# Attention and a feed-forward layer in one kernel: another order of seven products at the hand-over, and operands of the second token pair made earlier

## The chip, the cores and the metric

One core of one Trainium2 chip. The metric is the device time of one execution in microseconds: 650.89 us, the median of three runs of the kernel before (649.39, 650.89 and 652.63).

## The reference

```python
# attention, B=4 H=8 S=576 D=64
scores = q @ k.T / sqrt(D) + bias(h, i, j)     # bias: a small MLP of log1p|i-j| / log1p(max(i,1))
attn = softmax(scores); x = attn @ v           # regrouped to x[2304 tokens, 512]
# feed-forward, d_ff = 2048
h = x @ w_in                                   # 512 -> 2048
g = s * relu(h)**2 + b
out = g @ w_out                                # 2048 -> 512
```

All in float32; the weights come as 64-bit floats and are decoded on the chip.

## The kernel before

**Attention.** 16 pairs (a head and two batches) go through the chip in `step(n)`, five steps a pair. The program is written out by hand: each engine gets its instructions in the order in which the Python code issues them, and works them off in that order. Pair 15 is the last; its results reach x as `rb` tiles (L443, L444), which are stored and read back as the last input block.

**Feed-forward.** x stands transposed, features by tokens, in three token pairs p of 768 tokens (two chunks of 384). The hidden width is cut into four groups g. An item is (g, p); the order of items is (0,0), (0,1), (0,2), (1,2) and so on, 12 in all. For one item the 2x2 block product (features halved, tokens halved) is made with seven products in place of eight, on sums of blocks: `W_OPS` and `X_OPS` name the operands, S1 to S4 sums of weights, T1 to T4 sums of x. Every float32 operand is split into a high and a low part, so that a product is six matmuls of 128x384 (`product`, L625 to L637: three combinations, two feature blocks). An item has two halves s, each with the seven products on other weight columns. So an item is 14 slots: slot T does product `ORDER[i]` of half s with n, r = divmod(T, 14) and s, i = divmod(r, 7); from the second item on, slots with i = 1, 4 and 6 also do 12 matmuls each of the output projection of the half before (L741). The first item has no projections beside it. A product is added on one of four PSUM banks (`BANK`, L457): 1 and then 2 on "a", 5 and then 3 on "b", 6 on "c", 7 and then 4 on "d".

**The posts of a half** (`quad_posts`, L640) take the banks apart. In the names used below: *keep* (ACT, L657) copies bank a after product 1 and before product 2 is added to it; *u2* (DVE, L661) adds that copy to bank c; *v* (DVE, L666) adds u2 to bank b after product 5 and before product 3 is added to it; *c22* (DVE, L669) adds bank d after product 7 and before product 4 is added to it; *relu11* (ACT, L680) reads bank a after product 2. Relu, square, affine, high and low (L684 to L716) turn the four results into the high and low part of g.

**Making an operand of x** is a cast of two blocks to the high part on ACT (*x_hi*, L594, two instructions) and two subtractions for the low part on DVE (*x_lo*, L598); T sums are two more DVE instructions each (L585). `prep` does this for the seven operands of pair 0 while the last two steps of attention run; `fresh_x` (L1025) posts it for pair 1 into slots 6 to 14 and for pair 2 into slots 20 to 28. GpSimd makes pair 0's T sums.

**Order of work.** `at(slot, fn, prio)` collects the posts of a slot, and `fire(slot)` issues them after the slot's products, by priority: posts that free banks have 0, the other posts 1, making operands 2. A product, and a post, waits by semaphore for what it reads or overwrites. The first four products stand by hand between the last steps of attention (L990 to L998); the loop at L1104 goes on with slot 4. The SP queue issues the DMAs in program order, stores of made operands (L603) among them.

Space: `xp` holds seven operand buffers, an eighth (`x7`) is made once the attention's buffers are closed (L1000).

Of the kernel before, what the change touches and what calls it, by code (L numbers as in the profile page):

```python
# [26 lines left out]
def attention_moe(ctx, tc, q, k, v, w_in, w_out, dist, par, out):  # L27
# [310 lines left out]
    def probs_t(n):  # L338
        p, t = divmod(n, 5)
        if p not in pts:  # L340
            pts[p] = (ptp.tile([128, 4, 2, S], F32, tag="pt", name="pt"),
                      ptp.tile([128, S], F32, tag="ptr", name="ptr"))
# [113 lines left out]
    ORDER = (1, 6, 5, 7, 2, 3, 4)  # L456
# [98 lines left out]
    xo, free_x, x_free = {}, [], [[], None]  # L555
# [37 lines left out]
    def x_hi(p, m, e):  # L593
        nc.scalar.activation(xo[p, m][:, 0, e], x_view(p, X_OPS[m], e), AF.Copy)  # L594

    def x_lo(p, m, e, free):
        t = xo[p, m]
        nc.vector.tensor_tensor(t[:, 1, e], x_view(p, X_OPS[m], e), t[:, 0, e].bitcast(F32), op=ALU.subtract)  # L598
        if isinstance(X_OPS[m], str):
            used((p, X_OPS[m], e), free)  # L600
# [24 lines left out]
    def product(n, s, m, last):  # L625
        g, p = items[n]
        b = BANK[m]
        if m in (1, 5, 6, 7):
            banks[n, s, b] = ps_h.tile([128, 512], F32, tag="h", name="hps")
        ps = banks[n, s, b][:, 0:CH]  # L630
        first = m in (1, 5, 6, 7)
        for i in range(6):
            k, e = divmod(i, 3)
            w, x = ((0, 0), (0, 1), (1, 0))[e]
            nc.tensor.matmul(ps, w_ops[m][:, w, k, s], xo[p, m][:, x, k], start=(first and i == 0),  # L635
                             stop=(i == 5), skip_group_check=not first)
        if last:  # L637
            free_x.append(xo.pop((p, m)))

    def quad_posts(n, s):  # L640
# [69 lines left out]
        def low(fo, j):  # L710
# [35 lines left out]
    def acc_of(p, i):  # L746
        if p != 1:
            return mix["acc" if p == 0 else "acc2"][i][:, 0:DM]
        f = big.bitcast(F32)
        return f[:, i, 0:512] if i < 4 else f[:, 2 * i - 8:2 * i - 6, 512:768]  # L750
# [173 lines left out]
    pctx = ExitStack()  # L924
    ptp = pctx.enter_context(tc.tile_pool(name="ptp", bufs=2, side="right", reuse_waits="tile"))
    scratch = [ptp.tile([128, 512], F32, tag="ws", name=f"ws{i}", bufs=4) for i in range(4)]
# [40 lines left out]
    def prep(m):  # L967
        x_new(0, m)
        for e in range(2):
            x_hi(0, m, e)  # L970
        for e in range(2):
            x_lo(0, m, e, x_free[e])

    next(att)
    for a in range(KB):
        load_x(1, a, 0, 2 * CH if a < KB - 1 else CH)
    next(att)
    for i in range(3):
# [39 lines left out]
    x_free[:] = [[t[:, 0:CH] for t in mix[e]] for e in ("acc", "acc2")]  # L1018
# [6 lines left out]
    def fresh_x(n, q, free):  # L1025
        base = 14 * n
        for a in range(KB) if q > 1 else ():
            at(base + 2, lambda a=a: load_x(q, a))
        for o, name in ((6, "T1"), (7, "T2"), (9, "T3"), (12, "T4")):
            for e in range(2):  # L1030
                at(base + o, lambda name=name, e=e: x_sum(q, name, e, nc.vector, free))
        for i, m in enumerate(ORDER):
            o = base + (7 + i if i > 0 else 6)
            at(o, lambda m=m: x_new(q, m))
            for e in range(2):
                at(o, lambda m=m, e=e: x_hi(q, m, e))
            for e in range(2):
                at(o + 1, lambda m=m, e=e: x_lo(q, m, e, free))
            if isinstance(X_OPS[m], str):
                at(o + 2, lambda m=m: store_x(q, m))  # L1040

    def fresh_w(g):
# [36 lines left out]
        for name, o in (("S1", 35), ("S2", 35), ("S3", 38), ("S4", 40)):  # L1079
# [8 lines left out]
    fresh_x(0, 1, x_free[0])  # L1088
    fresh_x(1, 2, x_free[1])
# [87 lines left out]
```

## Time and profile before

| | us |
|---|---|
| median of three runs | 650.89 |
| the profiled execution | 650.64 |
| its span on the core | 648.9 |
| PE busy | 631.1 (97%) |
| DVE, ACT, POOL busy | 511.4, 450.9, 165.6 |

The page gives one execution. The busy shares are means over the attention (the first 262 us) and the feed-forward layer (the rest). PE is busy nearly all the time, so its idle stretches and the stretches at the lower TensorE clock are what is left to read; the 40 slices of the page show one place with both in mid-span, at the change from attention to feed-forward.

### The profile page before, as it was taken

Reading aid. Unit: us, or ns where it says so; the run is one execution under the profiler, and the core shown is the slowest. Engines: PE = TensorE matmul, PEld = TensorE weight load, DVE = VectorE, ACT = ScalarE, POOL = GpSimd, SP = SyncE. Lnnn points to the kernel's source line nnn. Section 1 sums busy time; section 2 is a strip of 40 time slices with the busy share of each in tenths; the row PEclk is TensorE's granted clock in tenths of the full one; section 3 lists DMA queues with packets and bytes.
Section 4 is the critical chain, followed back from the end, with each engine's and each line's share of the span. In section 5 each row is a group of like instructions: output and inputs, shape, how many; then the busy total and the mean of one; then the engine's idle time right before and its main releaser. Section 6 shows DMA issues by size and latency. Waiting matters only on the chain.

```text
span 648.9 us, 14523 instructions
## 1 busy us (share of the span) xinstructions
PE 631.1 (97%) x5418; PEld 511.6 (79%) x5418; DVE 511.4 (79%) x1093; ACT 450.9 (69%) x945; POOL 165.6 (26%) x196
## 2 busy tenths in 40 slices
PE   8999999999999999979999999999999999999997
PEld 5667666666666666879898899999888999998886
DVE  7988889999999988897887566698686698575542
ACT  7988787888888788687676685576574665655540
POOL 7991423345697524010010100010100100000000
PEclk9999999999999999979999999999999999999999
DMA  6988777775776565693522445421627210718112
GB/s 187 327 249 248 260 245 236 246 235 183 255 245 220 170 205 159 219 368 110 223 92 89 168 164 177 164 88 34 239 95 251 90 58 1 268 48 280 62 48 98
DMA packets 51058, 115.27 MB, mean 178 GB/s; under 512 B 10156, under 2 KB 18860, under 8 KB 50988
## 3 DMA queue, kind: packets, MB, share of 16 engines
q1 hardware_dynamic: 50652, 114.08, 52.6%
q8 instruction: 43, 0.70, 0.4%
q10 hardware_dynamic: 208, 0.26, 0.1%
q14 instruction: 27, 0.22, 0.1%
q0 software_dynamic: 128, 0.00, 0.0%
HBM read 83.59 MB, written 30.14 MB: 175 GB/s over the span
## 4 chain that ended last, share of the span: by engine, by line
PE 75%; DMA 7%; POOL 5%; ACT 5%; DVE 4%; issue 3%; SPq 1%; DVEq 0%; ACTq 0%; POOLq 0%
PE o L741 31%; PE hps L635 27%; PE bps L168 5%; PE xps L437 5%; PE sps L275 4%; PE tps L348 3%; ACT pr L308 3%; DMA qt<-in_q_dram 2%; DMA kt<-in_k_dram 2%; DVE tt L297 1%; DMA rs<-rt 1%; POOL kr L248 1%; DMA big<-in_moe_w_in_dram 1%; DVE pt L378 1%; ACT pt L376 1%
## 5 line engine op out<-in xcount | busy, mean ns | idle before, releaser
L741 PE MATMUL o<-wo,gt 128*128 128x512 f32 x864 | 209.2, 392 | 0.0
L635 PE MATMUL hps<-x,wi 128*128 128x384 f32 x1008 | 190.7, 340 | 3.3 <-DVE h L666 3.3
L635 PEld LDWEIGHTS hps<-x,wi 128*128 128x128 f32 x1008 | 180.8, 190 | 10.0 <-DVE h L666 3.6
L741 PEld LDWEIGHTS o<-wo,gt 128*128 128x128 f32 x864 | 161.2, 188 | 31.3
L308 ACT ACTIVATE pr<-tt,mn 128x576 f32<-128x576 f32 x144 | 110.7, 770 | 35.4 <-DVE mn L297 35.2
L297 DVE CUSTOM_DVE_ANT_0 tt<-sps,bt 128x576 f32<-128x576 f32 x128 | 91.4, 751 | 8.4 <-PE sps L275 6.7
L348 PEld LDWEIGHTS tps<-ident,pr 64*128 64x128 f32 x1216 | 44.8, 137 | 44.2 <-issue 18.7
L437 PE MATMUL xps<-pt,vt 128*64 128x256 f32 (+1 forms) x512 | 76.0, 418 | 1.0 <-PE xps L437 1.0
L275 PE MATMUL sps<-kr,qr 64*128 64x288 f32 x768 | 73.2, 307 | 1.0 <-POOL kr L248 0.8
L348 PE MATMUL tps<-ident,pr 64*128 64x64 f32 x1216 | 56.7, 229 | 5.2 <-ACT pt L376 2.8
L275 PEld LDWEIGHTS sps<-kr,qr 64*128 64x128 f32 x768 | 58.8, 186 | 2.4 <-POOL kr L248 1.0
L699 ACT ACTIVATE h<-h,sb 128x384 f32<-128x384 f32 x72 | 50.8, 706 | 12.0 <-DVE h L695 10.8
L493 POOL TENSOR_SCALAR wf<-wf 128x512 f32<-128x512 f32 x16 | 13.0, 813 | 160.8 <-ACT wf L491 160.6
L378 DVE COPY pt<-tps 128x512 f32<-128x512 f32 x64 | 43.9, 685 | 9.1 <-PE tps L348 8.8
L680 ACT ACTIVATE h<-hps 128x384 f32<-128x384 f32 x24 | 11.7, 487 | 54.5 <-PE hps L635 54.5
L437 PEld LDWEIGHTS xps<-pt,vt 128*64 128x64 f32 x512 | 31.3, 136 | 21.3 <-issue 9.4
L716 DVE TENSOR_TENSOR gt<-h,gt 128x384 fp32r<-128x384 f32 x72 | 40.0, 557 | 6.1 <-ACT gt L707 6.0
L168 PE MATMUL bps<-f,pt__125 128*32 128x79 f32 (+44 forms) x640 | 39.7, 390 | 2.0 <-POOL f L137 1.2
L707 ACT ACTIVATE gt<-h 128x384 fp32r<-128x384 f32 x72 | 37.9, 526 | 2.3
L135 DVE TENSOR_SCALAR f<-lg,thr 128x432 f32<-128x432 f32 (+9 forms) x68 | 39.3, 659 | 0.0
L168 PEld LDWEIGHTS bps<-f,pt__125 128*32 128x32 f32 x640 | 24.1, 109 | 17.7 <-issue 6.4
L376 ACT ACTIVATE pt<-tps 128x512 f32<-128x512 f32 x64 | 36.8, 575 | 0.0
(145 smaller groups left out, 823.6 us busy)
## 6 DMA issues: line engine op xcount, KB each, us to landing
x<-xs SPq DMA_DIRECT2D x24, 768.0 KB
bias<-stg SPq DMA_DIRECT2D x36, 295.5 KB
xs<-x SPq DMA_DIRECT2D x12, 768.0 KB
bt<-bias SPq DMA_DIRECT2D x7, 1152.0 KB
kt<-in_k_dram SPq DMA_DIRECT2D x16, 464.0 KB
wd<-in_moe_w_out_dram SPq DMA_DIRECT2D x12, 512.0 KB
x<-xt SPq DMA_DIRECT2D x28, 192.0 KB
qt<-in_q_dram SPq DMA_DIRECT2D x16, 320.0 KB
```

Source lines behind the costliest of these rows:

```text
L168: nc.tensor.matmul(pb[32 * c:32 * c + 32, base + a:base + b], w2bd, mov, start=True, stop=True)
L275: nc.tensor.matmul(o, a, b, start=(i == 0), stop=(i == 2))
L297: nc.vector.tensor_tensor_reduce(tt.rearrange("p (a b) -> p a b", a=2), ps[x][:, :, 0:HALF], bias.rearrange("p (a b) -> p a b", a=2), -1.0 ...
L308: nc.scalar.activation(pr[:, x], tts.pop((n, x)), AF.Exp, bias=mn[:, x:x + 1], scale=-1.0, accum_out=sums[p][:, col // 3, col % 3:col % 3 ...
L348: nc.tensor.matmul(outs[r], src[d], ident[d, d], is_transpose=True, start=start, stop=True, skip_group_check=not start)
L376: nc.scalar.activation(o, i, AF.Copy)
L378: nc.vector.tensor_copy(o, i)
L437: nc.tensor.matmul(o, vt[:, 4 * x + kb, :], pt[:, kb, x, c], start=(i == 0), stop=(i == 4))
L635: nc.tensor.matmul(ps, w_ops[m][:, w, k, s], xo[p, m][:, x, k], start=(first and i == 0), stop=(i == 5), skip_group_check=not first)
L699: return lambda: nc.scalar.activation(tmp[fo, j], tmp[fo, j], AF.Identity, bias=b_, scale=s_)
L716: nc.vector.tensor_tensor(lo, tmp[fo, j], hi, op=ALU.subtract)
L741: nc.tensor.matmul(os_t[t], gt[:, a, tok], w[:, b], start=(fo == 0 and i == 0), stop=(fo == 3 and i == 2))
```

## The change

The order of the seven products becomes 1, 6, 2, 5, 7, 3, 4, and the posts of a half move to new slots with it: keep stays in slot 1 of the half and u2 in 2, relu11 goes from 5 to 3, v from 3 to 4, c22 from 4 to 5. The operand of product 1 of pair 0 is made on GpSimd ahead of the last steps of attention. Two operand buffers ("guests") and x7 are made as soon as the buffer of attention pair 14 is free, for which the pool of these buffers is split in two. In them the operands 1, 5 and 2 of pair 1, and the sum T1, are made by hand between the first four products. What is left of pair 1 is posted into slots 4 to 11, each operand's casts and subtractions in one slot (`x_make`); pair 2 goes to slots 18 to 27, its loads from slot 16 to 14. When the guests are done their room takes accumulators of pair 2.

```diff
-    ORDER = (1, 6, 5, 7, 2, 3, 4)
+    ORDER = (1, 6, 2, 5, 7, 3, 4)
...
         return (
-            (1, 0, keep), (2, 0, u2), (3, 0, v), (4, 0, c22),
-            (5, 1, relu11), (5, 1, square11), (5, 1, relu(f1, 1)), (5, 1, square(f1, 1)),
-            (6, 0, c12), (6, 1, square_v(f0, 1)), (6, 1, affine(f1, 1)), (6, 1, high(f1, 1)), (6, 1, high(f0, 0)),
-            (7, 0, c21), (7, 1, low(f1, 1)), (7, 1, low(f0, 0)), (7, 1, affine(f0, 1)), (7, 1, high(f0, 1)),
-            (7, 1, relu(f1, 0)),
+            (1, 0, keep), (2, 0, u2), (3, 0, relu11), (4, 0, v), (5, 0, c22), (6, 0, c12), (7, 0, c21),
+            (3, 1, square11), (4, 1, high(f0, 0)),
+            (5, 1, low(f0, 0)), (5, 1, relu(f1, 1)), (5, 1, square(f1, 1)),
+            (6, 1, square_v(f0, 1)), (6, 1, affine(f1, 1)), (6, 1, high(f1, 1)),
+            (7, 1, low(f1, 1)), (7, 1, affine(f0, 1)), (7, 1, high(f0, 1)), (7, 1, relu(f1, 0)),
...
+    def x_make(q, m, free):
+        x_new(q, m)
+        for e in range(2):
+            x_hi(q, m, e)
+        for e in range(2):
+            x_lo(q, m, e, free)
+
+    prep(1, nc.gpsimd, nc.gpsimd)
     next(att)
...
-    for m in ORDER:
+    for m in ORDER[1:]:
         prep(m)
...
+    x_sum(1, "T1", 0, nc.vector, sums1)
+    x_sum(1, "T1", 1, nc.vector, sums1)
+    x_make(1, 1, sums1)
     next(att)
     store_xt(NP - 1)
     copy_x()
     fire(1)
-    product(0, 0, 5, False)
+    product(0, 0, ORDER[2], False)
     fire(2)
-    product(0, 0, 7, False)
+    x_make(1, 5, sums1)
+    product(0, 0, ORDER[3], False)
     fire(3)
-    pctx.close()
+    x_make(1, 2, sums1)
...
-    fresh_x(0, 1, x_free[0])
-    fresh_x(1, 2, x_free[1])
+    at(4, lambda: store_x(1, 5))
+    fresh_x(1, sums1, ((4, "T2"), (6, "T3"), (7, 6), (8, 7), (9, "T4"), (10, 3), (11, 4)))
+    for a in range(KB):
+        at(14, lambda a=a: load_x(2, a))
+    fresh_x(2, [t[:, 0:CH] for t in fulls + new_f],
+            ((18, "T1"), (18, 1), (19, "T2"), (20, 6), (21, 2), (22, 5), (23, "T3"), (24, 7), (25, "T4"), (26, 3), (27, 4)))
```

How the queues stand, at the three places that matter. In these rows `x_...` is an operand buffer, `acc_...` a T sum of pair 1, `wd` the input of pair 1, `hps` a bank.

DVE in the first half of the first item, before: the last subtractions of pair 0, the last eviction of attention (L443, L444), then u2 (L661), v (L666), c22 (L669).

```order
L598 TENSOR_TENSOR x_5186<-ws_1026,x_5186 128x384
L598 TENSOR_TENSOR x_5186<-h_5262,x_5186 128x384
L443 TENSOR_TENSOR rb<-xps,rb 128x256
L444 TENSOR_TENSOR rb<-xps,rb 128x320
L661 TENSOR_TENSOR h_5262<-hps,h_5262 128x384
L666 TENSOR_TENSOR h_5263<-hps,h_5262 128x384
L669 TENSOR_TENSOR h_5263<-hps,h_5263 128x384
L684 SCALAR_TENSOR_TENSOR h_5263<-h_5263,sb 128x384
```

The same place now (the lines are three further on: u2 is L664, v L669, c22 L672, the square L687).

```order
L586 TENSOR_TENSOR acc_5329<-wd 128x384
L586 TENSOR_TENSOR acc_5330<-wd 128x384
L599 TENSOR_TENSOR x_5272<-wd,x_5272 128x384 x2
L444 TENSOR_TENSOR rb<-xps,rb 128x256
L445 TENSOR_TENSOR rb<-xps,rb 128x320
L664 TENSOR_TENSOR h_5276<-hps,h_5276 128x384
L599 TENSOR_TENSOR x_5273<-acc_5329,x_5273 128x384
L599 TENSOR_TENSOR x_5273<-acc_5330,x_5273 128x384
L687 SCALAR_TENSOR_TENSOR h_5277<-h_5277,sb 128x384
L599 TENSOR_TENSOR x_5274<-wd,x_5274 128x384 x2
L669 TENSOR_TENSOR h_5277<-hps,h_5276 128x384
```

Four instructions came in ahead of the eviction, and four subtractions and the square between u2 and v; the two T2 sums and c22 follow v.

ACT from the relu after c22 of the first half (L687) to keep of the second half (L657), before.

```order
L687 ACTIVATE h_5263<-h_5263 128x384
L690 ACTIVATE h_5263<-h_5263 128x384
L699 ACTIVATE h_5263<-h_5263,sb 128x384
L707 ACTIVATE gt_5376<-h_5263 128x384
L705 ACTIVATE gt_5377<-h_5263,sb 128x384
L594 ACTIVATE x_5385<-wd 128x384 x2
L699 ACTIVATE h_5263<-h_5263,sb 128x384
L707 ACTIVATE gt_5378<-h_5263 128x384
L687 ACTIVATE h_5262<-h_5262 128x384
L657 ACTIVATE h_5261<-hps 128x384
```

The same place now (relu L690, keep L660).

```order
L690 ACTIVATE h_5277<-h_5277 128x384
L693 ACTIVATE h_5277<-h_5277 128x384
L702 ACTIVATE h_5277<-h_5277,sb 128x384
L710 ACTIVATE gt_5396<-h_5277 128x384
L702 ACTIVATE h_5277<-h_5277,sb 128x384
L710 ACTIVATE gt_5397<-h_5277 128x384
L690 ACTIVATE h_5276<-h_5276 128x384
L511 ACTIVATE x_5183<-acc_5331 128x384
L511 ACTIVATE x_5183<-acc_5332 128x384
L660 ACTIVATE h_5275<-hps 128x384
```

One high (L705) went out of the row; two casts stand in it as before, now of operand 6.

DVE in the second half of the first item from u2 (L661) to v (L666), before.

```order
L661 TENSOR_TENSOR h_5261<-hps,h_5261 128x384
L716 TENSOR_TENSOR gt_5379<-h_5262,gt_5379 128x384
L585 TENSOR_TENSOR acc_5391<-wd 128x384
L585 TENSOR_TENSOR acc_5392<-wd 128x384
L598 TENSOR_TENSOR x_5180<-acc_5389,x_5180 128x384
L598 TENSOR_TENSOR x_5180<-acc_5390,x_5180 128x384
L666 TENSOR_TENSOR h_5261<-hps,h_5261 128x384
```

The same place now, from the two subtractions ahead of u2 (L664) to v (L669).

```order
L599 TENSOR_TENSOR x_5184<-acc_5333,x_5184 128x384
L599 TENSOR_TENSOR x_5184<-acc_5388,x_5184 128x384
L664 TENSOR_TENSOR h_5275<-hps,h_5275 128x384
L719 TENSOR_TENSOR gt_5398<-h_5276,gt_5398 128x384
L586 TENSOR_TENSOR acc_5329<-wd,acc_5331 128x384
L586 TENSOR_TENSOR acc_5330<-wd,acc_5332 128x384
L687 SCALAR_TENSOR_TENSOR h_5275<-h_5275,sb 128x384
L599 TENSOR_TENSOR x_5185<-wd,x_5185 128x384 x2
L669 TENSOR_TENSOR h_5276<-hps,h_5275 128x384
```

Between u2 and v stood five instructions and now stand six; the two subtractions of operand 7 are ahead of u2, whose casts on ACT stand behind keep.

## Rows read from the trace of the kernel before

**Rows 1.** The page: busy time of PE, and the granted clock in 40 slices.

```profile
PE 631.1 (97%) x5418; PEld 511.6 (79%) x5418; DVE 511.4 (79%) x1093; ACT 450.9 (69%) x945; POOL 165.6 (26%) x196
...
PEclk9999999999999999979999999999999999999999
```

**Rows 2.** Waits of PE: line, who is waited for, total us, times, longest.

```profile
PE hps L635 <- DVE h L666: 3.3, 1, 3.3
```

**Rows 3.** Windows: length, busy PE, PEld, DVE, ACT, POOL; clock; DMA share, GB/s.

```profile
278.60:279.20 0.60, 0.00 (x0) 0.00 (x0) 0.60 (x2) 0.60 (x2) 0.00 (x0) 0.56 0.97 321
280.00:285.00 5.00, 5.00 (x17) 5.00 (x16) 4.97 (x11) 4.25 (x10) 0.00 (x0) 0.50 0.95 367
285.50:286.00 0.50, 0.50 (x5) 0.50 (x4) 0.50 (x2) 0.50 (x2) 0.12 (x1) 1.00 1.03 430
290.00:340.00 50.00, 50.00 (x253) 45.27 (x251) 40.78 (x80) 35.53 (x72) 5.17 (x6) 1.00 0.41 152
```

**Rows 4.** Timeline of PE: start, length, instruction, count, [idle before <- releaser].

```profile
265.20 0.96 PE L635 MATMUL hps<-x,wi 128*128 128x384 f32 x4
265.83 10.28 PE L635 MATMUL hps<-x,wi 128*128 128x384 f32 x57
274.79 1.00 PEld L635 LDWEIGHTS hps<-x,wi 128*128 128x128 f32 x6 [0.28 <-ACT h L657]
279.44 6.85 PE L635 MATMUL hps<-x,wi 128*128 128x384 f32 x22 [3.33 <-DVE h L666]
289.23 3.31 PE L635 MATMUL hps<-x,wi 128*128 128x384 f32 x18
```

**Rows 5.** Timeline of DVE at the hand-over.

```profile
257.68 1.02 DVE L598 TENSOR_TENSOR x<-big,x 128x384 fp32r<-128x384 f32 x2
...
265.32 0.42 DVE L443 TENSOR_TENSOR rb<-xps,rb 128x256 f32<-128x256 f32 x1 [1.00 <-PE xps L437]
...
266.06 0.55 DVE L661 TENSOR_TENSOR h<-hps,h 128x384 f32<-128x384 f32 x1
266.71 0.56 DVE L666 TENSOR_TENSOR h<-hps,h 128x384 f32<-128x384 f32 x1
...
269.22 0.62 DVE L684 SCALAR_TENSOR_TENSOR h<-h,sb 128x384 f32<-128x384 f32 x1 [1.07 <-ACT h L680]
...
278.83 0.55 DVE L666 TENSOR_TENSOR h<-hps,h 128x384 f32<-128x384 f32 x1
```

**Rows 6.** Timeline of ACT at the hand-over.

```profile
268.69 0.49 ACT L680 ACTIVATE h<-hps 128x384 f32<-128x384 f32 x1 [4.99 <-PE hps L635]
269.08 0.52 ACT L687 ACTIVATE h<-h 128x384 f32<-128x384 f32 x1
...
270.93 0.53 ACT L707 ACTIVATE gt<-h 128x384 fp32r<-128x384 f32 x1
271.36 0.60 ACT L705 ACTIVATE gt<-h,sb 128x384 fp32r<-128x384 f32 x1
271.87 0.92 ACT L594 ACTIVATE x<-wd 128x384 fp32r<-128x384 f32 x2
274.27 0.47 ACT L657 ACTIVATE h<-hps 128x384 f32<-128x384 f32 x1
```

**Rows 7.** Timeline of POOL before the hand-over, and of POOL and DVE in the second item.

```profile
252.02 0.72 PE L282 MATMUL sps<-kt,qt 64*64 64x288 f32 x8
252.24 1.00 POOL L585 TENSOR_TENSOR h<-big 128x384 f32<-128x384 f32 x1 [3.44 <-ACT pr L308]
255.84 1.00 POOL L585 TENSOR_TENSOR h<-big,h 128x384 f32<-128x384 f32 x1 [0.55 <-PE tps L348]
...
317.46 0.96 POOL L493 TENSOR_SCALAR wf<-wf 128x512 f32<-128x512 f32 x1 [2.44 <-ACT wf L491]
317.86 1.43 DVE L598 TENSOR_TENSOR x<-acd,x 128x384 fp32r<-128x384 f32 x2
```

**Rows 8.** Groups of POOL by form: count, busy us, mean ns.

```profile
L247 POOL TENSOR_SCALAR qr<-qt 128x512 fp32r<-128x512 f32 x16 | 9.9, 621 | 67.2 <-DMA qt<-in_q_dram 46.6 <-PE sps L275 16.8 <-PE tps L348 3.6
```

More of the change, by code (lines that the diff above doesn't have):

```diff
@@ L340, in probs_t @@
         if p not in pts:
-            pts[p] = (ptp.tile([128, 4, 2, S], F32, tag="pt", name="pt"),
-                      ptp.tile([128, S], F32, tag="ptr", name="ptr"))
+            pool = ptps[p % 2]
+            pts[p] = (pool.tile([128, 4, 2, S], F32, tag="pt", name="pt"),
+                      pool.tile([128, S], F32, tag="ptr", name="ptr"))
         pt, ptr = pts[p]
@@ L591, in x_new, with x_hi, x_lo @@
         xo[p, m] = free_x.pop(0)
-    def x_hi(p, m, e):
-        nc.scalar.activation(xo[p, m][:, 0, e], x_view(p, X_OPS[m], e), AF.Copy)
-    def x_lo(p, m, e, free):
+    def x_hi(p, m, e, engine=nc.scalar):
+        cast(engine, xo[p, m][:, 0, e], x_view(p, X_OPS[m], e))
+    def x_lo(p, m, e, free, engine=nc.vector):
         t = xo[p, m]
-        nc.vector.tensor_tensor(t[:, 1, e], x_view(p, X_OPS[m], e), t[:, 0, e].bitcast(F32), op=ALU.subtract)
+        engine.tensor_tensor(t[:, 1, e], x_view(p, X_OPS[m], e), t[:, 0, e].bitcast(F32), op=ALU.subtract)
         if isinstance(X_OPS[m], str):
@@ L637, in product @@
         if last:
-            free_x.append(xo.pop((p, m)))
+            t = xo.pop((p, m))
+            if not any(t is e for e in guests):
+                free_x.append(t)
     def quad_posts(n, s):
@@ L923, in attention_moe @@
     wf = wip.tile([128, 4, 512], F32, name="wf")
-    pctx = ExitStack()
-    ptp = pctx.enter_context(tc.tile_pool(name="ptp", bufs=2, side="right", reuse_waits="tile"))
-    scratch = [ptp.tile([128, 512], F32, tag="ws", name=f"ws{i}", bufs=4) for i in range(4)]
+    pctx = [ExitStack(), ExitStack()]
+    ptps = [None, pctx[1].enter_context(tc.tile_pool(name="pt1", bufs=1, side="right", reuse_waits="tile"))]
+    scratch = [ptps[1].tile([128, 512], F32, tag="ws", name=f"ws{i}", bufs=4) for i in range(4)]
+    ptps[0] = pctx[0].enter_context(tc.tile_pool(name="pt0", bufs=1, side="right", reuse_waits="tile"))
     free_f.extend(scratch[0:2])
@@ L977, in attention_moe @@
     next(att)
+    pctx[0].close()
+    op = ctx.enter_context(tc.tile_pool(name="op", bufs=1, reuse_waits="tile"))
+    free_x.append(op.tile([128, 2, 2, CH], F32R, name="x7"))
+    guests.extend(op.tile([128, 2, 2, CH], F32R, tag="q", name=f"x{8 + i}", bufs=2) for i in range(2))
     for i in range(3):
@@ L987, in attention_moe @@
     next(att)
-    for m in ORDER:
+    for m in ORDER[1:]:
         prep(m)
-    product(0, 0, 1, False)
-    product(0, 0, 6, False)
+    free_x.extend(guests)
+    mix["acc"] = [tp.tile([128, 640 if i < 3 else 576], F32, tag="vn" if i < 3 else "tt", name=f"acc{i}")
+                  for i in (0, 1, 3, 4, 5)]
+    sums1 = [t[:, 0:CH] for t in mix["acc"]]
+    product(0, 0, ORDER[0], False)
+    product(0, 0, ORDER[1], False)
+    x_sum(1, "T1", 0, nc.vector, sums1)
+    x_sum(1, "T1", 1, nc.vector, sums1)
+    x_make(1, 1, sums1)
     next(att)
@@ L1017, in attention_moe, with third_acc @@
     free_raw[:] = raws
-    x_free[:] = [[t[:, 0:CH] for t in mix[e]] for e in ("acc", "acc2")]
+    def third_acc():
+        mix["acc2"] = [op.tile([128, 3, DM], F32, tag="q", name=f"ad{i}", bufs=2) for i in range(2)]
+    at(26, third_acc)
     for n in range(1, NI + 1):
@@ L1023, in attention_moe, with fresh_x @@
                 at(14 * n + 7 * j + o, lambda n=n, j=j, t=t: evict(n - 1, 1 - j, t), 0)
[L1025 to L1040, printed above, removed]
+    def fresh_x(q, free, slots):
+        for o, e in slots:
+            if isinstance(e, str):
+                for x in range(2):
+                    at(o, lambda e=e, x=x: x_sum(q, e, x, nc.vector, free))
+            else:
+                at(o, lambda e=e: x_make(q, e, free))
+                if isinstance(X_OPS[e], str):
+                    at(o + 2, lambda e=e: store_x(q, e))
     def fresh_w(g):
@@ L1078, in fresh_w @@
                     at(o, lambda i=i: wout_lo(g, i, nc.vector), 1)
-        for name, o in (("S1", 35), ("S2", 35), ("S3", 38), ("S4", 40)):
+        for name, o in (("S1", 35), ("S2", 35), ("S3", 38), ("S4", 41)):
             at(base + o, lambda name=name: w_sum(name, nc.vector), 1)
```

30 lines of the change are left out of this document (15 added, 15 removed).

## The prediction

> **What bounds the kernel now.** I read the page first: PE is busy 97% of the span, and the granted clock leaves full speed in one slice in the middle [rows 1]. In the 50 us from 290 on PE has no idle time at all at full clock, while DVE and ACT have a fifth and more to spare [rows 3]: from there on the kernel is a row of matmuls, and nothing that changes on other engines is felt unless it makes PE wait. The waits of PE name one thing of size, 3.3 us on the DVE add v of line L666 [rows 2]. The timeline of PE puts it at 276.11 to 279.44, before product 3 in the second half of the first item, after 57 matmuls without a break but for one wait of 0.28 us on keep [rows 4]. The windows show what follows: the granted clock goes to 0.50 (1.2 GHz) within 278.60 to 279.20, is there until 285, and is 1.00 (2.4 GHz) again from 285.50 [rows 3]. At full clock a matmul of a product takes (10.28 - 0.28 - 3.31) / (57 - 18) = 0.172 us, a product 1.03 us; the 22 matmuls after the wait took 6.85 us where 22 x 0.172 = 3.78 would do, so the low clock cost 3.07 us [rows 4]. The whole place is worth 3.33 + 0.28 + 3.07 = 6.7 us, and that is all that the change can win.
>
> Why v was late is read from DVE and ACT. Both work their queues off in order, and in the first item no projections stand between the products: a slot is 1.03 us of PE, into which the posts of a half and the operands of pair 1 have to fit.
>
> **The first half.** DVE cannot start the last eviction of attention before PE has finished with it, at 265.32, and u2 followed at 266.06, v at 266.71 [rows 5]. PE started its next product at 265.20 [rows 4]; that is now product 2, then 5 and 7, and at 265.20 + 3 x 1.03 = 268.3 it comes to product 3, which needs v. Between u2 and v there now stand four subtractions and a square. Two subtractions take 1.02 us, each 0.55, so one frees DVE after 0.47; the square of 0.62 after 0.54 [rows 5]. v begins at 266.06 + 5 x 0.47 + 0.54 = 268.95 and ends at 269.50; PE went on 0.06 us after v's end before (278.83 + 0.55 to 279.44) [rows 4, 5], so it does at 269.56: a new wait of 1.3 us. The two T2 sums and c22 behind v end 3 x 0.47 = 1.41 after it, product 3 takes 1.03, so product 4 waits 0.4 more.
>
> **GpSimd.** It now makes operand 1 of pair 0 before the second-block T sums. The casts can begin when the last score matmuls, at 252.02 for 0.72 us, have let go of the room [rows 7]. Two casts of 384 columns cost 0.5 each at most (0.62 for 512 [rows 8]), the two subtractions 1.0 each like its sums [rows 7], so the four T sums, which ran from 252.24 to 256.84 [rows 7], now run from about 255.8 to 259.9. DVE starts its subtractions at 257.68 [rows 5], so 2.2 us lie beside each other. The trace has one such meeting: of two subtractions that began at 317.86 beside a GpSimd instruction of 317.46 to 318.42, 1.43 us came where 1.02 is usual [rows 5, 7]: the first ended 0.4 us late, as if it had begun when GpSimd ended. Taken so for every instruction, with GpSimd and DVE in turn, DVE gets two subtractions done by 260.8, where ACT's casts would have allowed six: 4 x 0.47 = 1.9 us behind. There is no idle time left before the eviction to catch up, as 12 + 2 sums + 2 subtractions take 7.5 us from 257.68 to 265.2. The ends are 0 and 2.2; I take 1.9, by the row of the same instruction. A rule of the Trainium skill bears on this, SBUF — State Buffer, Who interferes with whom: a Vector instruction with two SBUF inputs and a GpSimd instruction that reads SBUF exclude each other, one waits for the whole of the other. By that rule the 1.9 stands, without it the sum below would be 654.8; the row at 317.86 sides with the rule.
>
> What these four instructions free on ACT and DVE is taken by the same four for operand 1 of pair 1, in the same stretch; so keep of the first half comes when it did, and this part wins nothing.
>
> **The second half.** Product 2 used to be the fifth of a half, it is now the third, and it overwrites bank a, which keep must have read. The gap from c22 to keep on ACT is a chain of dependent work: from 269.08 to 274.27 + 0.47 it took 5.66 us before; one high has gone out of it, 271.36 to 271.87, two casts stand in it as before: 5.15 now [rows 6]. PE meanwhile has products 4, 1 and 6, 3.09 us. It waits 5.15 + 0.06 - 3.09 = 2.1 us. Before, it had two more products in hand there, and waited 0.28 [rows 4].
>
> Then v of the second half. The casts of operand 7 stand on ACT behind keep, square, affine and high, its subtractions on DVE in the same slot, ahead of u2. From keep's end: square and affine 1.3 (relu, square and affine took 269.08 to 270.93, the relu 0.55 of it), high 0.43 (270.93 to 271.36), first cast 0.5 (two 0.92) [rows 6]: the first subtraction starts after 2.2 us. Two subtractions, u2, a low, two T4 sums, the square, two subtractions and v follow: 6 x 0.47 + 0.54 + 2 x 0.47 + 0.55 = 4.85 us. v ends 7.05 after keep, PE has had products 2, 5 and 7 (3.09) and waits 7.11 - 3.15 = 4.0 us for product 3. That is longer than the 3.33 of before, so I let the clock cost the same 3.07 as then, after it; a wait of 0.4 before product 4 is hidden by the slow product 3 as before.
>
> **The rest at nothing.** Later items have 12 projection matmuls after the second, fifth and seventh product of a half, so keep and v have those between them and their product; if the spare fifth of DVE and ACT did not cover pair 2's earlier operands, PE would wait there as here. Pair 2's loads go two slots earlier, and so does their first use. SP issues the same stores, in another order.
>
> **The sum**, against the profiled execution of 650.64 (0.25 under the median): 650.64 - 3.33 - 0.28 + 1.3 + 1.9 + 0.4 + 2.1 + 4.0 = 656.7 us.
>
> **The rivals.**
> 1. It works as a relief. ACT sat idle 4.99 us before 268.69 and DVE 1.00 before 265.32 [rows 5, 6], and three operands are made early; if DVE and ACT gain enough on PE, all the waits go: 650.64 - 6.7 = 644.0. Against it: the early work stands on DVE between u2 and v, and DVE is the late engine. Chance 0.10.
> 2. The waits come without the collision, and are broken up by products so that the clock never falls: 656.7 - 1.9 - 3.07 = 651.7. For it: the clock fell only after 2.5 us without a matmul. Against: the last wait is longer than the one that lowered it. Chance 0.15.
> 3. The clock falls at more than one of the three waits, and a second low stretch costs as much as the first: 656.7 + 3.07 = 659.8. Against it: a slow product ahead of a wait is hidden by the wait. It is decided by whether the clock falls at the first, 3.2 us wait. Chance 0.13. The Trainium skill, TensorE: Matmul & The Clock Gate, A second HAM failure mode: psum-queue depth-cycling, says that short idle pieces between groups of matmuls let the clock go to and fro, which costs between the bursts; no stretch of this trace has several such pieces in a row.
>
> **How the numbers follow.** My forecast, 656.7, has 0.62, with 654 to 659 as its own range, from the collision at 0 or 2.2 us and where the clock turns. Half a percent, which is about what a measurement of this kernel can tell from no change, is 3.25 us: 647.6 to 654.1 counts as the same. Faster is rival 1, 0.10. Same is rival 2 and the low end of the forecast, 0.21. The rest, 0.69, is slower. The range that leaves out rival 1 and the high end of rival 3 is 650.5 to 660.5.
>
> **What would show it.** Right: the waits of PE name v twice (about 3 and 4 us) and keep once (about 2); DVE subtractions of 1 us or more beside GpSimd at 258 to 260; a low clock after the last wait; nothing new after 300. Wrong: PE without idle time from 265 to 300 (rival 1), waits of this size with the clock at 1.00 throughout (rival 2), or waits of PE in the second item, which I have at nothing.

## The result and the profile after

The kernel after takes 654.93 us (median of six runs, 653.87 to 656.73), the kernel before 650.38 in the same session: a ratio of 1.0071 with a 95% interval of 1.0048 to 1.0095, slower by 4.6 us. The profiled execution took 654.26 us, its span 652.1.

The page of after, to be laid beside [rows 1]: PE is as busy as before, and two slices are below full clock at the place where one was.

```profile
PE 632.1 (97%) x5418; PEld 511.3 (78%) x5418; DVE 515.2 (79%) x1091; ACT 454.0 (70%) x943; POOL 168.0 (26%) x200
...
PEclk9999999999999999889999999999999999999999
```

The waits of PE (line, who is waited for, total, times, longest), where [rows 2] had one wait for v:

```profile
PE hps L636 <- DVE h L669: 6.0, 2, 3.6
PE hps L636 <- ACT h L660: 0.2, 1, 0.2
```

The timeline of PE, against [rows 4]. L636 is `product`, L744 the projections.

```profile
260.49 2.37 PE L636 MATMUL hps<-x,wi 128*128 128x384 f32 x12
263.91 3.40 PE L636 MATMUL hps<-x,wi 128*128 128x384 f32 x18
269.71 6.38 PE L636 MATMUL hps<-x,wi 128*128 128x384 f32 x24 [2.41 <-DVE h L669]
276.30 3.40 PE L636 MATMUL hps<-x,wi 128*128 128x384 f32 x18 [0.20 <-ACT h L660]
283.29 6.35 PE L636 MATMUL hps<-x,wi 128*128 128x384 f32 x24 [3.60 <-DVE h L669]
289.48 0.86 PE L744 MATMUL o<-wo,gt 128*128 128x512 f32 x3
```

Product 3 waits for v in both halves, product 2 of the second half hardly for keep. The same 24 matmuls take 4.79 us at full clock in order_only below; here they take 6.38 and 6.35. The windows of after say why: the granted clock is at 0.50 (1.2 GHz) after each of the two long waits, for 3.4 us each time, and at 1.00 (2.4 GHz) between; in [rows 3] it fell once, for 6.8 us.

```profile
271.50:274.50 3.00, 3.00 (x11) 3.00 (x11) 2.97 (x7) 2.87 (x6) 0.00 (x0) 0.50 0.99 401
275.00:280.00 5.00, 4.50 (x25) 3.85 (x23) 3.10 (x7) 4.92 (x12) 0.00 (x0) 1.00 0.99 287
285.00:288.00 3.00, 3.00 (x11) 3.00 (x11) 2.21 (x5) 2.90 (x6) 0.29 (x1) 0.50 1.02 422
```

The last three T sums on the timeline of GpSimd, where [rows 7] had sums of 1.00 us only:

```profile
255.52 1.00 POOL L586 TENSOR_TENSOR h<-big,h 128x384 f32<-128x384 f32 x1
256.47 1.33 POOL L586 TENSOR_TENSOR h<-big 128x384 f32<-128x384 f32 x1
257.76 1.32 POOL L586 TENSOR_TENSOR h<-big,h 128x384 f32<-128x384 f32 x1
```

The timeline of DVE, against [rows 5]: its first subtraction of pair 0, two longer steps beside GpSimd, the eviction (L444), u2 (L664) and v (L669) of the first half, and the step that holds u2 of the second half up.

```profile
256.39 0.55 DVE L599 TENSOR_TENSOR x<-ws,x 128x384 fp32r<-128x384 f32 x1
257.11 1.11 DVE L599 TENSOR_TENSOR x<-h,x 128x384 fp32r<-128x384 f32 x1 [0.17 <-ACT x L511]
258.15 1.82 DVE L599 TENSOR_TENSOR x<-big,x 128x384 fp32r<-128x384 f32 x2
...
265.52 0.41 DVE L444 TENSOR_TENSOR rb<-xps,rb 128x256 f32<-128x256 f32 x1
...
266.25 0.54 DVE L664 TENSOR_TENSOR h<-hps,h 128x384 f32<-128x384 f32 x1
...
269.11 0.55 DVE L669 TENSOR_TENSOR h<-hps,h 128x384 f32<-128x384 f32 x1
...
278.40 1.03 DVE L599 TENSOR_TENSOR x<-acc,x 128x384 fp32r<-128x384 f32 x2 [1.42 <-ACT x L511]
279.35 0.55 DVE L664 TENSOR_TENSOR h<-hps,h 128x384 f32<-128x384 f32 x1
...
282.69 0.55 DVE L669 TENSOR_TENSOR h<-hps,h 128x384 f32<-128x384 f32 x1
```

ACT, against [rows 6]: the relu after c22 (L690), keep (L660), and the casts of operand 7 (L511) for which DVE stands idle.

```profile
271.10 0.52 ACT L690 ACTIVATE h<-h 128x384 f32<-128x384 f32 x1 [2.19 <-DVE h L672]
...
275.77 0.47 ACT L660 ACTIVATE h<-hps 128x384 f32<-128x384 f32 x1
...
277.86 0.92 ACT L511 ACTIVATE x<-acc 128x384 fp32r<-128x384 f32 x2
```

How to compare executions: up to the first product the program of all kernels from early_only to filled is nearly the same, yet the first product began anywhere between 259.94 and 265.31 us of the span. So the kernels are compared by the *stretch*, from the first product to the first projection (both starts on PE's timeline), and the *rest*, from there to the end of the span. For before these two rows, and the 24 matmuls after its wait, are

```profile
261.77 2.38 PE L635 MATMUL hps<-x,wi 128*128 128x384 f32 x12
...
279.44 7.20 PE L635 MATMUL hps<-x,wi 128*128 128x384 f32 x24 [3.33 <-DVE h L666]
286.47 2.92 PE L741 MATMUL o<-wo,gt 128*128 128x512 f32 x12
```

| kernel | ratio to before, 95% | waits in the stretch, us | low clock there, us | stretch, us | rest, us |
|---|---|---|---|---|---|
| before | 1 | 0.28, 3.33 | 6.8 | 24.70 | 362.4 |
| after | 1.0071 (1.0048 to 1.0095) | 2.41, 0.20, 3.60 | 6.8 | 28.99 | 362.6 |
| order_only | 1.0005 (0.9984 to 1.0026) | 1.67, 2.70 | none | 23.38 | 362.9 |
| early_only | 1.0051 (1.0034 to 1.0069) | 0.95, 0.20, 4.21 | 6.8 | 26.56 | 362.3 |
| no_meeting | 1.0056 (1.0031 to 1.0081) | 0.94, 1.77, 2.02 | 6.8 | 27.39 | 362.5 |
| filler | 1.0080 (1.0056 to 1.0104) | 0.34, 1.76 | none | 27.43 | 363.6 |
| v_first | 1.0070 (1.0047 to 1.0092) | 0.53, 4.89, 1.15 | 6.8 | 28.32 | 362.6 |
| op7_late | 1.0059 (1.0035 to 1.0083) | 2.42, 0.21, 1.78 | 6.8 | 26.83 | 363.6 |
| early_late | 1.0037 (1.0012 to 1.0062) | 0.95, 0.20, 1.46 | none | 22.28 | 366.2 |
| spread | 1.0061 (1.0034 to 1.0088) | 1.61, 1.41, 2.15 | 3.4 | 25.67 | 364.6 |
| early_late2 | 0.9990 (0.9969 to 1.0011) | 0.96, 0.20, 1.44 | 3.4 | 23.83 | 362.3 |
| both_late | 0.9999 (0.9978 to 1.0019) | 2.42, 0.79, 0.82 | 3.4 | 24.81 | 363.1 |
| less_dve | 1.0106 (1.0077 to 1.0134) | 0.56, 0.72, 1.77, 2.65 | 3.4 | 26.64 | 365.6 |
| filled | 0.9966 (0.9942 to 0.9990) | 0.20 | none | 22.29 | 362.4 |

The waits are idle times of PE's matmuls; only the 0.28 of before is taken from the weight loads [rows 4]. Stretch and rest of after are 4.29 + 0.2 us over those of before, nearly all that the medians differ by. Nearly the whole loss is in the stretch.

One more number is of use below. The 24 matmuls after the wait of before took 7.20 us, and 4.80 at full clock in filled, so the low clock cost before 2.40 us. An estimate of its stretch at full clock is 24.70 - 2.40 = 22.30 us.

### The profile page after: what moved, and what is told of

Same layout as the page of the kernel before. It is cut to its first block, busy times and chain, and to the rows that moved or that the text cites. A ratio compares the mean times of both kernels' runs of the same rounds, so it can differ in the third digit from the quotient of the medians.

```text
span 652.1 us, 14493 instructions
## 1 busy us (share of the span) xinstructions
PE 632.1 (97%) x5418; PEld 511.3 (78%) x5418; DVE 515.2 (79%) x1091; ACT 454.0 (70%) x943; POOL 168.0 (26%) x200
## 4 chain that ended last, share of the span: by engine, by line
PE 56%; DVE 1%; issue 0%
PE o L744 30%; PE hps L636 25%; DVE x L599 0%; DVE acc L766 0%; DVE h L687 0%; DVE h L672 0%; DVE acc L586 0%; DVE h L669 0%
## 5 line engine op out<-in xcount | busy, mean ns | idle before, releaser
L744 PE MATMUL o<-wo,gt 128*128 128x512 f32 x864 | 209.2, 392 | 0.0
L636 PE MATMUL hps<-x,wi 128*128 128x384 f32 x1008 | 192.2, 341 | 6.4 <-DVE h L669 6.0
L636 PEld LDWEIGHTS hps<-x,wi 128*128 128x128 f32 x1008 | 181.0, 191 | 14.4 <-DVE h L669 6.6
L744 PEld LDWEIGHTS o<-wo,gt 128*128 128x128 f32 x864 | 161.2, 188 | 31.3
L494 POOL TENSOR_SCALAR wf<-wf 128x512 f32<-128x512 f32 x16 | 11.4, 713 | 162.0 <-ACT wf L492 161.6
L690 ACT ACTIVATE h<-h 128x384 f32<-128x384 f32 x48 | 24.9, 519 | 23.6 <-DVE h L672 21.4
```

The source lines that it names most:

```text
L744: nc.tensor.matmul(os_t[t], gt[:, a, tok], w[:, b], start=(fo == 0 and i == 0), stop=(fo == 3 and i == 2))
```

## The experiments

**order_only**: the order of products and its posts, put into the kernel before.

```diff
-    ORDER = (1, 6, 5, 7, 2, 3, 4)
+    ORDER = (1, 6, 2, 5, 7, 3, 4)
...
```

> The kernel before with the new order of products and the new slots of the posts alone; no operand is made early and GpSimd makes none. My theory (waits come from what stands ahead of v and keep on DVE and ACT): no wait in the first half, where nothing but the square stands between u2 and v; about 2.1 us before product 2 of the second half on keep (as in the sum of the prediction), about 3 us before product 3 on v, one low stretch of the clock: 652.5 us, +2 against before. Rival A (the order costs nothing, the operands made early are the whole loss): 650.4. Rival B (the order is the whole loss): 654.9.

PE's timeline of order_only:

```profile
273.50 3.42 PE L635 MATMUL hps<-x,wi 128*128 128x384 f32 x18 [1.67 <-ACT h L657]
279.62 4.79 PE L635 MATMUL hps<-x,wi 128*128 128x384 f32 x24 [2.70 <-DVE h L666]
```

The two waits are there nearly as expected (1.67 and 2.70 for 2.1 and 3), but this execution had no low clock: 0.76 us of waits more than before, 2.4 us of slow products less (24 matmuls in 4.79 for 7.20). No change is measured, and rival A holds for the order: by itself it costs nothing that can be told. In this execution the waits it brings and the clock it was spared cancel: at full clock on both sides its stretch is 23.38 for 22.30.

**early_only**: the early operands with the old order.

```diff
-    ORDER = (1, 6, 2, 5, 7, 3, 4)
+    ORDER = (1, 6, 5, 7, 2, 3, 4)
...
```

> The changed kernel with the old order of products and the old slots of the posts; the operands made early, the guests and the operand split on GpSimd stay. My theory: the first half waits for v as in the changed kernel, but behind two subtractions in place of four, so about 1.6 us; keep of the second half has two more products in hand and costs under 0.7; v of the second half about 4 us; the clock falls twice: 653.0 us, +2.6 against before. Rival A (the early operands are the whole loss): 654.9. Rival B (they cost nothing): 650.4.

```profile
268.05 6.89 PE L636 MATMUL hps<-x,wi 128*128 128x384 f32 x36 [0.95 <-DVE h L669]
...
280.68 6.34 PE L636 MATMUL hps<-x,wi 128*128 128x384 f32 x24 [4.21 <-DVE h L669]
```

The median is 653.03 us where my theory had 653.0; against before in the same session it is +3.3 for +2.6. The last wait is 4.21 for 4, the first 0.95 for 1.6, and the clock fell once, for 6.8 us, not twice. Most of the loss comes with the early operands and the posts that were moved for them. The order on top takes the ratio from 1.0051 to 1.0071, but these two intervals overlap.

**no_meeting**: GpSimd and DVE kept apart.

```diff
-    prep(1, nc.gpsimd, nc.gpsimd)
+    x_new(0, 1)
+    for e in range(2):
+        x_hi(0, 1, e, nc.gpsimd)
+        load_tokens(xo[0, 1][:, 1, e].bitcast(F32), e, 0, CH)
```

> The changed kernel, in which GpSimd makes only the two casts of operand 1 of pair 0; in place of its low part two DMAs bring the plain x (so product 1 of pair 0 has another low part). GpSimd ends its T sums 2 us earlier, before DVE begins its subtractions, so the two engines do not meet. My theory: no DVE subtraction over 0.6 us and no GpSimd sum over 1.05 us there, the eviction 1.1 us earlier, the first wait for v 1.3 us in place of 2.41: 653.8 us, 1.1 under the changed kernel. Rival A (the meeting costs nothing, the queue alone makes v late): 654.9, first wait still 2.4. Rival B (with the shorter first wait the clock does not fall there, and its cost comes back too): 652 or less.

DVE's timeline of no_meeting begins the same work 0.73 us later than after (257.12 for 256.39), as PE its first product (261.22 for 260.49), and yet reaches the eviction 0.76 us earlier:

```profile
257.12 0.55 DVE L599 TENSOR_TENSOR x<-ws,x 128x384 fp32r<-128x384 f32 x1
257.59 0.55 DVE L599 TENSOR_TENSOR x<-h,x 128x384 fp32r<-128x384 f32 x1
...
264.76 0.42 DVE L444 TENSOR_TENSOR rb<-xps,rb 128x256 f32<-128x256 f32 x1
```

PE's timeline of no_meeting:

```profile
268.98 4.82 PE L636 MATMUL hps<-x,wi 128*128 128x384 f32 x24 [0.94 <-DVE h L669]
```

From the first subtraction to the eviction it is 7.64 us, with the meeting 9.13. There it follows PE's last attention matmul, which ends at 264.72, at once. So the meeting is real and costs 1.49 us, more than the 1.1 that I expected, and the first wait fell by as much, 1.47, from 2.41 to 0.94. Of rival B only the half is right: the clock did not fall at the first wait, but it did after the next one, and keep's wait came back to 1.77. The stretch is 1.60 us shorter. The median, 653.84, is where my theory had it, but the intervals of the ratios, 1.0056 and 1.0071, overlap, so a gain of the whole is not shown.

**filler**: PE kept busy in the two long waits.

```diff
+        if T in (5, 12):
+            idle = ps_o.tile([128, DM], F32, tag="o", name="idle")
+            for _ in range(12 if T == 5 else 20):
+                nc.tensor.matmul(idle[:, 0:CH], w_ops[1][:, 0, 0, 0], xo[0, 3][:, 0, 0], start=True, stop=True)
```

> The changed kernel with matmuls that nobody reads in the two waits before product 3: 12 of 128x384 in the first half (2.1 us at full clock), 20 in the second (3.5 us). The waits stay, the engine is busy in them. My theory: the clock stays at 1.00; the products between are fast again, so the wait for keep comes back, from 0.2 to about 2 us, and what is won is the last low stretch alone, about 1.7 us: 653.2 us. Rival A (each low stretch costs what the one of before did, 3.07 us, as in the prediction's third rival): 6 us won, 648.8. Rival B (the low clock hides wholly in the waits): 654.9.

```profile
270.11 2.25 PE L1135 MATMUL idle<-x,wi 128*128 128x384 f32 x12
272.70 4.82 PE L636 MATMUL hps<-x,wi 128*128 128x384 f32 x24 [0.34 <-DVE h L669]
279.28 3.39 PE L636 MATMUL hps<-x,wi 128*128 128x384 f32 x18 [1.76 <-ACT h L660]
282.51 3.63 PE L1135 MATMUL idle<-x,wi 128*128 128x384 f32 x20
...
301.38 0.79 PE L636 MATMUL hps<-x,wi 128*128 128x384 f32 x3 [0.57 <-DVE h L672]
```

In the stretch all is as expected: clock at 1.00, 24 matmuls in 4.82, keep's wait back at 1.76, 1.56 us won. But the second item gave 1.0 of it back (rest 363.6; the wait for c22 at 301.38 is new), and the median shows no gain. That fits a low clock under which DVE and ACT could catch up; it was not shown apart.

**v_first**: the work between u2, v and c22 of the first half put behind c22.

```diff
-    x_make(1, 5, sums1)
     product(0, 0, ORDER[3], False)
     fire(3)
-    x_make(1, 2, sums1)
...
-    fresh_x(1, sums1, ((4, "T2"), (6, "T3"),
+    fresh_x(1, sums1, ((5, 5), (5, 2), (5, "T2"), (6, "T3"),
```

> The changed kernel with the making of operands 5 and 2 of pair 1 and the T2 sums taken out from between u2, v and c22 of the first half and posted behind c22 (slot 5). Nothing is left out, the work on DVE and ACT is the same. Theory A (the place in DVE's queue is the loss): the first wait falls from 2.41 to under 0.5, the others stay, one low stretch goes: 652 us. Theory B (DVE and ACT have a fixed amount of work between the hand-over and the second item, and a wait taken away in one place comes back in the next): the first wait goes as well, but the four casts and six DVE instructions now stand ahead of keep of the second half, whose wait grows from 0.2 to between 3 and 5 us; v's wait stays at 3.5 to 4: 654.5 us, as the changed kernel.

```profile
269.50 4.46 PE L636 MATMUL hps<-x,wi 128*128 128x384 f32 x24 [0.53 <-DVE h L669]
278.85 5.84 PE L636 MATMUL hps<-x,wi 128*128 128x384 f32 x18 [4.89 <-ACT h L660]
```

Theory B in the main: the first wait went, keep's wait grew to 4.89, and the time is that of after. Only v's wait, for which B had 3.5 to 4, fell to 1.15. Moving the work inside the first item moves the wait.

**op7_late**: operand 7 of pair 1 made four slots later.

```diff
-((7, 6), (8, 7), (9, "T4"), (10, 3), (11, 4))
+((7, 6), (9, "T4"), (10, 3), (12, 7), (12, 4))
```

> The changed kernel with operand 7 of pair 1 made in slot 12 in place of 8 and operand 4 in slot 12 in place of 11. In the changed kernel DVE stood 1.42 us idle for operand 7's casts with u2 behind it. Theory A (that blocked queue is the last wait): u2 of the second half follows keep at once, the wait for v falls from 3.60 to 1.5 to 2 us and the second low stretch gets shorter or goes: 652.5 us. Theory B (the amount of work alone counts): the last wait gets shorter, but c22 and the posts behind it wait instead, in the second half and the second item: 654.5 us.

```profile
282.07 6.00 PE L636 MATMUL hps<-x,wi 128*128 128x384 f32 x24 [1.78 <-DVE h L669]
...
298.47 1.31 PE L636 MATMUL hps<-x,wi 128*128 128x384 f32 x6 [0.67 <-DVE h L672]
```

Both theories in part: the last wait is halved, as A has it, and 1.0 us comes back in the second item, as B has it. As a whole it can't be told from after (1.0059 and 1.0071).

**early_late**: the old order, and all that is left of pair 1 made later.

```diff
-((7, 6), (8, 7), (9, "T4"), (10, 3), (11, 4))
+((7, 6), (10, 7), (11, "T4"), (12, 3), (12, 4))
```

> As early_only (old order of products, three operands early, GpSimd makes operand 1 of pair 0), but what is left of pair 1 is made later: operand 7 in slot 10 in place of 8, T4 in 11 for 9, operand 3 in 12 for 10, operand 4 in 12 for 11; they are first needed in slots 17, 19 and 20. Theory A (operands made ahead of v of the second half are what makes v late; the second item has room): waits of 0.9 and about 1.8 us for v, no low clock: 649 us, under the kernel before. Theory B (the amount of work): 653 as early_only.

The stretch, 22.28, is the shortest of all so far, but the rest lost 3.8 us. ACT's timeline of early_late shows to what: the first cast of pair 2, posted into slot 18, holds ACT up until pair 2's input has come. SP issues these loads behind the stores of pair 1's last operands, from 288.20 to 299.24 us here and from 283.36 to 293.58 in early_only.

```profile
299.98 0.53 ACT L511 ACTIVATE x<-wd 128x384 fp32r<-128x384 f32 x1 [6.47 <-DMA wd<-xt]
```

**spread**: T1, T3 and four low parts of pair 1 on GpSimd, each operand near its slot.

```diff
+    sums_at = (('T1', 1, 1), ('T2', 5, 0), ('T3', 7, 1), ('T4', 10, 0))
+    ops_at = ([3, 3, 1], [8, 10, 1], [6, 6, 1], [13, 13, 0], [12, 12, 0], [8, 9, 1], [10, 11, 0])
```

> A version meant to be better: old order of products; all operands of pair 1 posted one by one between slots 3 and 13, each near the slot that needs it, and GpSimd, idle here, makes T1, T3 and the low parts of operands 1, 6, 5 and 2 of pair 1; v posted one slot earlier, some posts of a half shifted by one slot. If DVE's amount of work is what the waits come from (14 of its 36 instructions here go to GpSimd) and the meeting of GpSimd and DVE costs under half of their time together, as seen after the change: waits of about 2 us in sum, no low clock, 646.5 us. If the meeting costs the whole of it: 650 us or more.

A miss: waits of 1.61, 1.41 and 2.15, and 1.74 more in the second item. The meeting was taken too cheaply in the expectation: on the timelines of spread a subtraction beside GpSimd takes 1.35 us (DVE at 257.61) for 0.55 alone, and two sums beside DVE take 2.61 (GpSimd at 258.51) for about 2.0. The branch of the expectation for a meeting that costs the whole, 650 us or more, is what came. How much of the waits it made was not taken apart; that giving DVE's work to GpSimd must pay is not borne out.

**early_late2**: early_late with pair 2 from slot 20 on (in this kernel and in both_late product 4 of pair 2 has other numbers, as the expectation of filled tells).

```diff
-            ((18, "T1"), (18, 1), (19, "T2"), (20, 6), (21, 2), (22, 5), ...
+    sum_at(2, 20, "T1", sums2)
+    op_at(2, 1, 20, 20, sums2)
...
```

> As early_late, with the operands of pair 2 made in slots 20 to 32 in place of 18 to 27. In early_late the stretch from the first product to the first projection took 22.28 us (24.70 before the change), but ACT then stood 6.47 us and DVE 4.32 us idle for pair 2's loads with evictions and posts behind them, and PE waited 1.38 and 1.25 us after 305. Theory A (only these posts stood too early): the 22.3 us stay, no wait after 290, 2.4 us under the kernel before: 647.6 us. Theory B (DVE's amount of work in the second and third item, with the decoding of weights): waits of 1 to 2 us come back after 290 in other places: 650 us.

```profile
280.57 6.36 PE L636 MATMUL hps<-x,wi 128*128 128x384 f32 x24 [1.44 <-DVE h L669]
```

The rest is back at 362.3 without a wait: pair 2's posts had been the loss of early_late. The waits of the stretch are those of early_late to 0.02 us, yet here the clock fell after them (282.0 to 285.5), and the stretch is 1.55 us longer.

**both_late**: the changed order with the posts of early_late2.

> The changed kernel (its order of products, its early operands) with the posts of early_late2: operand 7 of pair 1 in slot 10, T4 in 11, operands 3 and 4 in 12, pair 2 in slots 20 to 32. It completes the square of order and posts. Theory A (the posts were the loss, the order costs nothing): 647.6 us, as early_late2. Theory B (in the new order keep and v of a half have fewer products in hand): waits of about 2 us before product 3 in the first half, up to 2 for keep and 1.2 for v in the second, 1 more in the second item: 651 us.

The waits are near theory B's, 2.42 and 0.79 and 0.82, with 0.50 in the second item; stretch and rest are 1.8 us over early_late2, but the ratios 0.9999 and 0.9990 can't be told apart. With the posts mended, the changed kernel's order is level with the kernel before.

**less_dve**: six subtractions left out.

```diff
+        if q == 1 and m in (1, 2, 3):
...
+            for e in range(2):
+                load_tokens(xo[q, m][:, 1, e].bitcast(F32), 2 * k - 2 + e, t0, t0 + CH)
+            return
```

> The changed kernel without the six subtractions that make the low parts of operands 1, 2 and 3 of pair 1 on DVE; DMAs bring the plain x in their place (so pair 1's products have other low parts). Two of the six stand ahead of the eviction, two between u2 and v of the first half, two ahead of v of the second. ACT's work is the same. Theory A (DVE's amount of work is what all the waits come from): 6 x 0.47 = 2.8 us come back: 652 us, first wait 0.5, last wait 1.5 or less. Theory B (in the second half DVE waits for ACT's casts with u2 behind them): the first wait goes to 0.5, the waits for keep and for v of the second half stay at 2 and 3 us: 654 us.

```profile
277.62 3.40 PE L636 MATMUL hps<-x,wi 128*128 128x384 f32 x18 [1.77 <-ACT h L660]
283.67 6.17 PE L636 MATMUL hps<-x,wi 128*128 128x384 f32 x24 [2.65 <-DVE h L669]
...
302.16 1.31 PE L636 MATMUL hps<-x,wi 128*128 128x384 f32 x6 [2.58 <-DVE h L672]
```

In the stretch it is theory B: the first wait goes to 0.56, keep's is 1.77 (0.20 in after), v's of the second half 2.65; 2.35 us come back there. As a whole it is inconclusive, since the added loads stand in SP's queue and pair 2's come later: ACT waited 3.27 us for them, and product 4 of the second item 2.58.

**filled**: early_late2 with matmuls that nobody reads in its two waits, and with T4 of pair 2 in another room.

```diff
+            for _ in range(5 if T == 5 else 8):
+                nc.tensor.matmul(idle[:, 0:CH], ...
...
```

> Meant to be better than both kernels: early_late2 with T4 of pair 2 kept in the room of pair 2's accumulators, which are not yet in use (in early_late2 and both_late the decoding of the next weights overwrote T4 before operand 4 was made from it, so pair 2's product 4 had wrong numbers there), and with matmuls that nobody reads in the two waits before product 3: 5 of 128x384 in the first half (0.86 us of a wait of 0.96), 8 in the second (1.38 of 1.44). In early_late2 the clock fell for 3.4 us after these waits, in early_late with the same waits it did not. Theory A (idle PE there is what lets the clock fall, and nothing waits behind): 22.3 us from the first product to the first projection and 362.4 from there to the end, 2.4 us under the kernel before: 648 us, a ratio of 0.9963. Theory B (what the clock takes comes back as a wait elsewhere, as with the fillers in the changed kernel): 0.999, as early_late2.

```profile
269.63 1.03 PE L1166 MATMUL idle<-x,wi 128*128 128x384 f32 x5
...
277.87 1.31 PE L636 MATMUL hps<-x,wi 128*128 128x384 f32 x6 [0.20 <-ACT h L660]
279.02 1.55 PE L1166 MATMUL idle<-x,wi 128*128 128x384 f32 x8
280.65 4.80 PE L636 MATMUL hps<-x,wi 128*128 128x384 f32 x24
```

648.63 us, a ratio of 0.9966 (0.9942 to 0.9990): theory A, to 0.1 us in the stretch (22.29) and in the rest (362.4). It is faster than both kernels, by 0.3% than before. That the clock stays up is borne out over all executions: the mean granted clock was 0.999 or more in ten of its twelve, 1.0 in four of the twelve of early_late2, and never over 0.997 in the seventeen of before in the same session. The ratios of filled and early_late2 themselves overlap.

The gain over before is the clock's and not that of the early operands: at full clock the stretch of before is an estimated 22.30 us, that of filled 22.29, of early_late 22.28. Before with such matmuls in its wait of 3.33 us might be as fast as filled; it was not run.

## Why the prediction was right, and which of its terms were not

The forecast was +6.1 us over the profiled execution by new waits for v, keep and v; it was +3.6 there, and +4.6 between the medians. The mechanism held: late posts on DVE and ACT behind early operands, and the two engines' meeting. The collision, keep and the clock had the wrong size, and part of the errors cancelled.

- **v of the first half behind five instructions**: 2.89 us from u2's start to v's, forecast; 266.25 to 269.11, 2.86, measured. Right.
- **GpSimd and DVE**: place, sign and manner were right, the size was 0.4 us too large. The sum of 256.47 met the subtraction of 256.39, which ended at 256.94, and took 0.33 us more than alone. The subtraction of 257.11 met that sum, which ended at 257.80: 0.56 more. The sum of 257.76 met that subtraction, which ended at 258.22: 0.32 more. The two subtractions from 258.15 met that sum, which ended at 259.08: 0.80 more. Each lost the time from its own start to the end of the other's instruction (0.47, 0.69, 0.46 and 0.93) less 0.13 or 0.14: the two engines took whole instructions in turn, as the prediction had it. The row at 317.86 fits too (0.56 less 0.15 is 0.41). The rule of the Trainium skill (SBUF — State Buffer, Who interferes with whom), that such two instructions exclude each other, agrees with these rows. The number of turns was off by one: after ran 1.28 us ahead of before at the first product, and at 260.8 less 1.28 DVE had finished three subtractions (the third at 259.5, an estimate: 259.97 less 0.47), not two of six. The meeting made the eviction 1.49 us later (no_meeting), in place of 1.9.
- **The first wait**: 1.3 + 1.9 forecast; 0.94 without the meeting (no_meeting) and 1.47 by it, 2.41 in sum, measured. In the 1.3 the three products before the wait are taken at 3.09 us; they took 3.40.
- **Product 4 of the first half**: 0.4 forecast. The weight loads of after (PEld, idle time in brackets) show it:

```profile
271.12 4.66 PEld L636 LDWEIGHTS hps<-x,wi 128*128 128x128 f32 x18 [0.40 <-DVE h L672]
```

- **keep**: the chain on ACT from the relu at 271.10 to keep's end at 276.24 took 5.14 us for a forecast of 5.15, but PE waited 0.20 for a forecast of 2.1. The step that failed is that PE would do products 4, 1 and 6 in 3.09 us. The clock had fallen at the first wait already, and the slow products filled the time; with the clock up the wait is there (1.76 in filler, 1.77 in no_meeting).
- **v of the second half**: from keep's end to v's end 7.00 us, forecast 7.05; the wait was 3.60 for 4.0.
- **The clock**: it fell twice, as in the third rival, and did not cost twice 3.07. Against 4.80 us at full clock (filled) the two groups of 24 lost 1.58 and 1.55, 3.13 in sum; the one of before lost 2.40 by the same measure, so its 3.07 was also taken 0.7 too high (22 matmuls at 0.172 us leave out the wait for c22 and the end of the last one). My sentence against that rival, that a slow product ahead of a wait is hidden by the wait, is what happened. The Trainium skill (TensorE: Matmul & The Clock Gate, A second HAM failure mode: psum-queue depth-cycling) tells of such a to and fro from short idle pieces between groups. The windows of after show one, behind waits of 2.41 and 3.60 us; early_late, with waits of 0.95, 0.20 and 1.46, had none.
- **The rest at nothing**: 0.2 us.

With the terms as measured, -3.33 - 0.28 + 2.41 + 0.40 + 0.20 + 3.60 + (3.13 - 2.40) = 3.7 us of the 4.29 in the stretch. The remaining 0.6 is the pieces: the row of 60 matmuls of before stands in three now, and a piece takes about 0.3 us more than its matmuls at 0.172 (18 in 3.40 for 3.10). So the forecast was 0.8 too high on the first wait, 1.9 on keep and 0.4 on v, and 1.3 too low by what the clock took more than before and by the pieces, which both stood in it at nothing; that these partly cancel is luck. The +3.6 of the profiled executions is lower still because after came to its first product 1.28 us sooner than before, and that start differs by up to 5 us between executions of nearly the same program.

The prediction had named the place in the queues; the runs tell what it takes to be rid of it. Parts taken alone say, by their ratios: the order +0.3 us (no change), the early operands with their posts +3.3. In the second half the casts and subtractions of operand 7 stood ahead of u2, and DVE stood idle 1.42 us for them; posting it later (op7_late, and early_late against early_only) takes half or more off the last wait. Within the first item, a wait taken away at one place returned at the next (v_first, filler). With work moved out of the first item, and pair 2's casts behind their loads, the stretch has no price behind it (early_late2), and there keeping the clock up paid (filled). But at equal clock that stretch is no shorter than the one of before, so no run shows that making operands early won anything.

## What to carry to other kernels

Before operands are made early, look at what stands behind them in each in-order queue: a cast that waits for its input holds up every post behind it, and the idle time that looked free is paid for one slot later. A post belongs as late as its reader allows, and behind the post that frees a bank. Slow products and waits cover each other, so price them together. Here filling the waits to keep the clock paid where the engines that are waited for were not behind themselves (filled), and not where they were (filler). And take a gain apart before it is put down to the change: what filled won is the clock that before had lost.

## What the runs showed of the hardware

- The same waits (0.95, 0.20 and 1.46 us in early_late; 0.96, 0.20 and 1.44 in early_late2) left the clock at 2.4 GHz in one execution and were followed by 1.2 GHz in the other: 24 matmuls in 4.81 and 6.36 us. The idle times alone do not tell whether the clock falls.
- GpSimd and DVE, both on operands in SBUF, took whole instructions in turn: each lost the time to the end of the other's instruction less 0.13 or 0.14 us, a sum on GpSimd 1.33 us for 1.00, a subtraction on DVE 1.11 for 0.55. In spread, where they met for longer, subtractions took 1.35.
- Before the first product nearly the same program differs by up to 5 us between executions (260.30 us in early_only, 265.31 in early_late), so spans of single executions hide effects of this size. Behind it waits repeat to hundredths where the code is the same: the first wait is 2.41, 2.42 and 2.42 in after, op7_late and both_late.
